# Frequency-domain filter and GELU layer on one core: second weights issued behind batch 1's input, first part of the filters' return at slot 10, last stage of batch 1 two slots later in shorter steps

## The chip, the core and the metric

The kernel runs on one core of a Trainium2 chip. The core has five engines that run side by side and meet only through semaphores: TensorE (PE, matrix products; PEld is its weight load), VectorE (DVE), ScalarE (ACT), GpSimd (POOL) and SyncE (SP). SP and POOL also issue transfers between the device memory and the on-chip memory; 16 DMA engines carry them out. The metric is the device time of one execution in microseconds (us), the median of several runs. Less is better.

## The reference, cut to what matters

Each of 8 batches of 3008 x 256 values goes through a filter in the frequency domain along the sequence; the result goes through two dense layers with an exact GELU between them.

```python
def _attn_ref(x, filt_r, filt_i):          # x: 8 x 3008 x 256
    X = np.fft.rfft(x, axis=1)
    F = (filt_r + 1j * filt_i)[None, :, :]
    return np.fft.irfft(X * F, n=x.shape[1], axis=1)

def _moe_ref(x, w_in, w_out):              # x: 24064 x 256, w_in: 256 x 2048, w_out: 2048 x 256
    h = x @ w_in
    g = 0.5 * h * (1.0 + erf(h * np.float32(1.0 / np.sqrt(2.0))))
    return g @ w_out
```

## The kernel before, in words

The sequence of 3008 is split as 47 x 64, so that the transform becomes four small stages of matrix products, s1 to s4, with a product by the filter F after s2. Between s1 and s2, and between s3 and s4, the data change their layout by a trip through device memory. For batches 1 to 7 the functions are:

- `load_x(b)` (L86): the batch's input, eight transfers issued by POOL, into a single buffer `x_sb`.
- `s1(b, c)`, c = 0 to 3 (L387): reads a quarter of the input. Each quarter reads two of the eight transfers. Results are copied to `a_sb` by DVE and ACT and written to a scratch tensor R by four transfers of SP (L396).
- `r1(b, c)` (L402): reads R back, one transfer of SP a quarter, into `b_sb`. Every r1 needs all sixteen writes of s1.
- `s2(b, p)`, p = 0 to 11 (L410, L413): two products of a pair of frequencies (k = 2p and 2p + 1), then DVE multiplies by F for these k.
- `s3(b, u)` and `s3_out` (L427, L439): three groups of four pairs; the results go to a second scratch tensor by SP.
- `r2(b, c)` (L446): two transfers of SP a quarter, back into `d_sb`.
- `s4(b, grp, half)` (L455, L299): sixteen units; unit u reads quarter u // 4. The results are the batch's sequence, in a ring that the dense layers read.

Batch 0 goes through its own variants (c1 to c4), ahead of everything else.

The dense layers run over 47 tiles of 512 rows. Time is cut into slots, sixteen a tile. In slot s, tile t = s // 16 does one sixteenth of the first product, `mm1` (L569), followed by GELU on ACT (L572), and the tile before does one sixteenth of the second product, `mm2` (L596) or, for most tiles, `mm2_seven` (L657). The latter computes the product with seven quarter products in place of eight; it needs sums of quarters of g (DVE: L627, L633, L640), sums of quarters of w_out (`weight_sums`, POOL, L613), and combines the results on DVE (L670 to L680). `put(slot, f, ...)` writes down by hand that f is issued at the head of a slot; every engine carries out its instructions in the order of issue. The mixing stages of batch b are spread over slots in this way, so that they run beside the dense layers of the batch before. For batch 1 the line

```python
s1, n1, r1, s2, n2, group, r2, s4, n4 = 0, 4, 15, 25, 2.5, 12, 62, 68, 0.72
```

gives: s1 at slots 0, 4, 8 and 12; the first three r1 at 15, the fourth at 33; s2 of pair p at `25 + 12 * (p // 4) + int(2.5 * (p % 4))`, so pairs 0 to 3 at 25 to 32 and pair 4 at 37; the first three r2 at 62; s4 of unit u at `68 + int(0.72 * u)`, that is 68 to 78; the fourth r2 three slots after the first s4. Tile 5 reads batch 1's first rows from slot 80.

Filters: `load_filters` (L95, POOL) loads F as batch 0 needs it, on 64 partitions. `dup_filters` (L113) copies pairs of k to the other 64 partitions. `save_filters` (L99, SP) writes F to the scratch tensor Fd, and `load_filters_again(k0, k)` (L107, SP) brings it back for k0 to k0 + k - 1 in the order of partitions that batches 1 to 7 need: eight transfers of 16 partitions each. The first return is for k 0 to 7 (128 KB a transfer), the second, put at slot 16, for k 8 to 23 (256 KB a transfer).

POOL's order ahead of the slots is: tables, input of batch 0, filters, w_in (L129), copies of F for k 4 to 11, w_out in two halves (`load_w_out`, L133), copies for k 12 to 23, small tables, input of batch 1. Behind that come, at slots 0 to 15, `table_2_parities`, `table_u_pick`, `table_4_rows`, `weights_4`, `weight_sums` and `table_4_all` (L371, L373), and at slot 25 the input of batch 2, not gated.

SP's order is: save of F, first return, sixteen writes of s1, three r1, second return, two stores of the first output tile (L604), the fourth r1, then s3's writes and stores by turns.

The product of batch 0 by F (L499) reads the copies that POOL makes; the product of batch 1 by F (L413) reads the returns. w_out is first read by POOL in `weight_sums` and by PE at slot 16.

Of the kernel before, what the change touches and what calls it, by code (L numbers as in the profile page):

```python
# [693 lines left out]
def kernel(  # L694
# [9 lines left out]
    m = _Mix(ctx, tc, x, filt_r, filt_i, moe_w_in, moe_w_out, out)  # L704
    nc, B, S = tc.nc, m.B, m.S
# [36 lines left out]
    m.load_w_in()  # L742

    nc.gpsimd.memset(m.vt[:, :, 96, :], 0.0)
    m.dup_filters(nc.gpsimd, 4, 8)
    m.load_w_out(0)
    m.load_w_out(8)
    m.dup_filters(nc.gpsimd, 12, 12)
    m.save_filters()


# [52 lines left out]
    m.table_u_rows(g)  # L804
    m.table_1_tiles(g)
    m.load_x(1)
    m.load_filters_again(0, 8)

    warm = g.tile([128, 1], FP32, name="warm")
    nc.scalar.activation(out=warm, in_=m.p, func=AF.Gelu)  # L810
# [11 lines left out]
    def put(slot, f, *a):  # L822
        at.setdefault(slot, []).append((f, a))

    def first(b):
        return (b * S // TCH) * 16

    for b in range(1, B):
        hi = first(b)
        if b == 1:  # L830
            s1, n1, r1, s2, n2, group, r2, s4, n4 = 0, 4, 15, 25, 2.5, 12, 62, 68, 0.72
        else:
            s1, n1, r1, s2, n2, group, r2, s4, n4 = hi - 94, 3.7, hi - 80, hi - 71, 3.4, 14, hi - 25, hi - 17, 1
        unit = lambda p: s2 + group * (p // 4) + int(n2 * (p % 4))
        for u in range(16):
            put(s4 + int(u * n4), m.s4, b, u // 2, u % 2)
        for c in range(4):
            put(s1 + int(c * n1), m.s1, b, c)
            put(r1 if c < 3 else unit(3) + 1, m.r1, b, c)
            put(r2 if c < 3 else s4 + int(4 * n4) + 1, m.r2, b, c)  # L840
        for p in range(12):
            put(unit(p), m.s2, b, p)
            if p % 4 == 3:
                put(unit(p) + 3, m.s3, b, p // 4)
                put(unit(p) + 4, m.s3_out, b, p // 4, 1)
        if b + 1 < B:
            for i in range(8):
                put(unit(i + 2) if b > 1 else 25, m.load_next, b, i + 2, i // 2, i % 2)
# [2 lines left out]
    put(1, m.table_u_pick, g)  # L851
    put(1, m.table_4_rows, g)
    put(1, m.weights_4, g)
    put(16, m.load_filters_again, 8, 16)
    put(4, m.weight_sums)
    put(12, m.table_4_factors, g)
# [48 lines left out]
```

## Time and profile before

| What | Value |
|---|---|
| median of 9 runs | 763.97 us (761.71 to 768.27) |
| profiled execution | 763.81 us, of which span 762.0 us |
| granted TensorE clock, mean | 0.996 |
| busy, share of span: PE / DVE / ACT / POOL | 97% / 76% / 72% / 15% |
| DMA issues F<-Fd: first return / second return | 8 x 128 KB, median 10.2 us to landing / 8 x 256 KB, 13.1 us |
| DMA issue w_out_sb | 2 x 512 KB, median 16.6 us to landing |
| DMA issue Fd<-F | 1 x 1536 KB, 11.3 us to landing |

The span runs from the first to the last instruction in one profiled execution. Busy time is that of the engine; waits and the issue of transfers are not in it. A tag such as `[4.51 <-DMA x_sb<-in_x_dram]` behind a row says how long the engine stood idle before it and what ended that.

### The profile page before, as it was taken

To read this page: it belongs to the slowest core of one execution; us is meant where nothing else is said; L and a number is where in the kernel's file an instruction comes from. 1 tells how busy PE (TensorE), PEld (TensorE's weight loads), DVE (VectorE), ACT (ScalarE), POOL (GpSimd) and SP (SyncE) were. 2 spreads that over 40 slices of the span, in tenths; PEclk is the share of its full clock that TensorE was granted. 3 is DMA by queue.
4 is the path that set the end of the run, shared out by engine and by line. 5 is a ranking of instruction groups with operands and counts; after the bars stand their busy time and mean duration, and the time that the engine had idled before them with its cause. 6 is when DMAs were issued, how large, how long until landed. Compare 5 with 4: busy or idle time off the path is not lost.

```text
span 762.0 us, 20182 instructions
## 1 busy us (share of the span) xinstructions
PE 739.8 (97%) x8388; PEld 518.5 (68%) x8388; DVE 581.8 (76%) x1043; ACT 547.5 (72%) x967; POOL 111.6 (15%) x207
## 2 busy tenths in 40 slices
PE   7969889999999999999999999999999999999998
PEld 4726556666777667676677666766767766777776
DVE  7834887799777986889778897779977799666562
ACT  7867567767787677867778666776678767777773
POOL 7779600012000210002000120001200000000000
PEclk9989999999999999999999999999999999999999
DMA  9998944555624655347535475264562523501011
GB/s 143 223 183 171 195 115 118 161 115 102 166 71 133 147 117 118 92 129 165 119 80 142 134 137 121 79 172 108 108 158 65 148 78 89 134 29 57 29 56 56
DMA packets 91500, 90.70 MB, mean 119 GB/s; under 512 B 7633, under 2 KB 78417, under 8 KB 91089
## 3 DMA queue, kind: packets, MB, share of 16 engines
q1 hardware_dynamic: 83024, 73.43, 36.2%
q0 software_dynamic: 8384, 16.00, 14.3%
q8 instruction: 65, 1.06, 0.6%
q14 instruction: 27, 0.21, 0.1%
HBM read 57.15 MB, written 48.23 MB: 138 GB/s over the span
## 4 chain that ended last, share of the span: by engine, by line
PE 81%; DMA 7%; DVE 6%; POOL 2%; issue 1%; ACT 1%; SPq 0%; DVEq 0%; POOLq 0%; ACTq 0%
PE ps_h L569 37%; PE ps_o L657 33%; DMA x_sb<-in_x_dram 3%; PE ps_s L455 3%; PE ps_s L427 2%; DVE p L413 2%; PE ps_s L387 2%; DVE s_sb L627 2%; PE ps_s L410 2%; DMA d_sb<-R 1%; DMA R<-v_sb 1%; PE ps_o L596 1%; POOL F L113 1%; DMA b_sb<-R 1%; ACT g_sb L572 1%
## 5 line engine op out<-in xcount | busy, mean ns | idle before, releaser
L572 ACT ACTIVATE g_sb<-ps_h 128x512 f16<-128x512 f32 x752 | 448.1, 598 | 187.0 <-PE ps_h L569 184.4
L569 PE MATMUL ps_h<-y_sb,w_in_sb 128*128 128x512 bf16 (+3 forms) x1600 | 447.3, 367 | 1.1 <-ACT g_sb L572 0.6
L657 PEld LDWEIGHTS <-g_sb 128*128 128x128 f16 x2880 | 190.2, 98 | 80.8 <-issue 15.2
L657 PEld LDWEIGHTS <-s_sb 128*128 128x128 f16 x2160 | 147.4, 98 | 51.5 <-issue 3.3
L569 PEld LDWEIGHTS <-w_in_sb 128*128 128x128 bf16 x1600 | 125.0, 98 | 9.7 <-issue 4.4
L657 PE MATMUL ps_o<-w_sums,g_sb 128*128 128x128 f16 x1440 | 125.0, 219 | 1.7 <-DVE g_sb L633 1.5
L657 PE MATMUL ps_o<-w_sums,s_sb 128*128 128x128 f16 x1440 | 124.5, 219 | 0.0
L627 DVE TENSOR_TENSOR s_sb<-g_sb 128x1024 f16<-128x1024 f16 x180 | 120.8, 694 | 0.0
L657 PE MATMUL ps_o<-w_out_sb,g_sb 128*128 128x128 f16 x1440 | 118.4, 219 | 0.4
L413 DVE TENSOR_TENSOR p<-ps_s,F 128x1024 bf16<-128x1024 f32 x84 | 102.6, 1221 | 18.5 <-PE ps_s L410 15.4
L118 POOL COPY gate<-p 1x1 bf16<-1x1 bf16 x40 | 19.4, 484 | 418.6 <-DVE p L413 418.6
L633 DVE TENSOR_TENSOR g_sb<-s_sb,g_sb 128x1024 f16<-128x1024 f16 x90 | 63.1, 701 | 1.1
L657 PE MATMUL ps_o<-w_out_sb,s_sb 128*128 128x128 f16 x720 | 62.2, 219 | 0.0
L640 DVE TENSOR_TENSOR s_sb<-g_sb 128x1024 f16<-128x1024 f16 x90 | 61.4, 682 | 0.0
L297 DVE CAST a_sb<-ps_s 128x512 bf16<-128x512 f32 x56 | 36.1, 686 | 24.7 <-PE ps_s L387 22.9
L299 DVE TENSOR_SCALAR y_sb<-ps_s 128x376 bf16<-128x376 f32 x56 | 30.6, 546 | 31.8 <-PE ps_s L455 31.7
L455 PEld LDWEIGHTS <-d_sb 96*128 96x128 bf16 x448 | 31.3, 98 | 29.0 <-issue 4.4
L675 DVE TENSOR_TENSOR t_sb<-t_sb,ps_o 128x256 f32<-128x256 f32 x45 | 18.7, 417 | 37.9 <-PE ps_o L657 37.8
L672 DVE TENSOR_TENSOR ost<-t_sb,ps_o 128x256 f32<-128x256 f32 x45 | 18.8, 419 | 31.2 <-PE ps_o L657 31.2
L455 PE MATMUL ps_s<-T4a,d_sb 96*128 96x94 bf16 x448 | 37.2, 206 | 3.0 <-DMA d_sb<-R 3.0
L680 DVE TENSOR_TENSOR ost<-t_sb,ps_o 128x256 f32<-128x256 f32 x90 | 33.6, 415 | 6.8 <-PE ps_o L657 6.8
L295 ACT ACTIVATE a_sb<-ps_s 128x512 bf16<-128x512 f32 x56 | 30.6, 608 | 6.3 <-PE ps_s L387 6.3
(149 smaller groups left out, 524.5 us busy)
## 6 DMA issues: line engine op xcount, KB each, us to landing
out_dram<-ost SPq DMA_DIRECT2D x93, 256.0 KB, 2.6
x_sb<-in_x_dram POOLq DMA_DIRECT2D x64, 188.0 KB, 3.9
R<-a_sb SPq DMA_DIRECT2D x112, 96.0 KB, 2.2
b_sb<-R SPq DMA_DIRECT2D x28, 384.0 KB, 4.4
R<-v_sb SPq DMA_DIRECT2D x84, 128.0 KB, 2.5
d_sb<-R SPq DMA_DIRECT2D x56, 192.0 KB, 4.0
F<-Fd SPq DMA_DIRECT2D x8, 256.0 KB, 13.1
Fd<-F SPq DMA_DIRECT2D x1, 1536.0 KB, 11.3
```

The lines of the kernel that those rows point to most:

```text
L295: self.nc.scalar.activation(out=out, in_=in_, func=AF.Copy, scale=1.0 if scale is None else scale)
L297: self.nc.vector.tensor_copy(out=out, in_=in_)
L299: self.nc.vector.tensor_scalar(out=out, in0=in_, scalar1=scale, scalar2=None, op0=ALU.mult)
L413: nc.vector.tensor_tensor(out=w, in0=ps.unsqueeze(1).to_broadcast([128, 2, 512]), in1=self.F[:, :, 2 * p:2 * p + 2, :].rearrange("p t a b ...
L455: nc.tensor.matmul(ps[:, 94 * i:94 * i + 94], lhsT=d[:, (grp % 2) * 4 + i, 128 * half:128 * half + 128], rhs=self.T4a[:, 4 * grp + i], sta ...
L569: nc.tensor.matmul(ps[:, o:o + n], lhsT=self.w_in_sb[:, dc, jc * 128:jc * 128 + 128], rhs=self.ring[:, dc, off:off + n], start=(dc == 0), ...
L572: nc.scalar.activation(out=self.st["g", t][:, jc, :], in_=ps, func=AF.Gelu)
L627: self.nc.vector.tensor_tensor(out=self.st["s", t][:, i:i + 2], in0=a, in1=b, op=ALU.subtract)
L633: self.nc.vector.tensor_tensor(out=a21[:, k], in0=self.st["s", t][:, k, 0], in1=a22[:, k], op=ALU.add)
L640: self.nc.vector.tensor_tensor(out=self.st["s4", t][:, k], in0=a12[:, k], in1=s2[:, k], op=ALU.subtract)
L657: nc.tensor.matmul(ps[:, (m + 1) % 2, sub, :], lhsT=a[:, i, 128 * sub:128 * sub + 128], rhs=b[:, i], start=i == 0, stop=i == 7)
L680: v(out=c(h, 1 - h), in0=tt, in1=p, op=ALU.add)
```

## The change

Three edits. The two halves of w_out are no longer issued between the copies of F but behind the input of batch 1, and the copies become one run of ten. The first return leaves its place behind the input of batch 1 and is put at slot 10; on SP it then stands behind the third group of s1's writes and ahead of the fourth. For batch 1, s4 starts at slot 70 with steps of 0.62, in place of 68 and 0.72: its units go to slots 70 to 79, its fourth r2 to slot 73.

```diff
     nc.gpsimd.memset(m.vt[:, :, 96, :], 0.0)
-    m.dup_filters(nc.gpsimd, 4, 8)
-    m.load_w_out(0)
-    m.load_w_out(8)
-    m.dup_filters(nc.gpsimd, 12, 12)
+    m.dup_filters(nc.gpsimd, 4, 20)
     m.save_filters()
...
     m.load_x(1)
-    m.load_filters_again(0, 8)
+    m.load_w_out(0)
+    m.load_w_out(8)
...
         if b == 1:
-            s1, n1, r1, s2, n2, group, r2, s4, n4 = 0, 4, 15, 25, 2.5, 12, 62, 68, 0.72
+            s1, n1, r1, s2, n2, group, r2, s4, n4 = 0, 4, 15, 25, 2.5, 12, 62, 70, 0.62
...
     put(1, m.weights_4, g)
+    put(10, m.load_filters_again, 0, 8)
     put(16, m.load_filters_again, 8, 16)
```

## The prediction, made before the changed kernel ran

> **What bounds the kernel now.** I read the busy slices of the page first: TensorE (PE) is busy 97% of the 762.0 us span, and the slices below 9 lie in the first sixth. The table by stage then shows which stretches lose time.
>
> ```profile
> core 0: us, PE busy (x) PEld busy (x) DVE busy (x) ACT busy (x) POOL busy (x), PEclk, DMA share, GB/s
> 40.00:50.00 10.00, 4.80 (x20) 1.48 (x24) 1.40 (x3) 2.95 (x6) 7.08 (x22) 0.66 1.12 205
> 110.00:120.00 10.00, 7.80 (x101) 5.77 (x99) 5.38 (x11) 6.01 (x12) 0.00 (x0) 1.00 0.89 208
> ```
>
> Two holes: 5.2 us at 40 to 50, where the granted clock also falls to 0.66 while the DMA engines are full, and 2.2 us at 110 to 120. The PE timeline names what ended each.
>
> ```profile
> 38.24 1.45 PE L546 MATMUL ps_c<-T4c,d_sb 96*128 96x94 bf16 x24
> 44.20 0.60 PE L387 MATMUL ps_s<-x_sb,T1s 47*64 47x512 bf16 x1 [4.51 <-DMA x_sb<-in_x_dram]
> 45.80 1.07 PE L387 MATMUL ps_s<-x_sb,T1s 47*64 47x512 bf16 x7 [0.99 <-DMA x_sb<-in_x_dram]
> ...
> 114.89 0.51 PE L455 MATMUL ps_s<-T4a,d_sb 96*128 96x94 bf16 x8 [2.19 <-DMA d_sb<-R]
> ```
>
> Batch 0's mixing is done at 39.69, and the first matmul of s1 (slot 0) waits 4.51 + 0.99 = 5.50 us for batch 1's input. Slot 68's s4 then waits until its rows are read back. The POOL timeline shows why the input is late.
>
> ```profile
> 22.08 1.79 POOL L133 DMA_DIRECT2D w_out_sb<-in_moe_w_out_dram  x2
> 23.86 5.94 POOL L113 COPY F<-F 64x1024 bf16<-64x1024 bf16 x6
> ...
> 30.86 3.05 POOL L86 DMA_DIRECT2D x_sb<-in_x_dram  x6
> 36.63 0.51 POOL L86 DMA_DIRECT2D x_sb<-in_x_dram  x1 [2.72 <-DMA w_out_sb<-in_moe_w_out_dram]
> 42.27 0.51 POOL L86 DMA_DIRECT2D x_sb<-in_x_dram  x1 [5.14 <-DMA w_out_sb<-in_moe_w_out_dram]
> ```
>
> The input stands behind w_out, which lands 19.0 us after its second issue, at 42.0, and shares the engines with the filters' first return. The last two lines also show that a POOL transfer waits for the landing of the eighth before it. Last, SyncE's queue (SP) and VectorE (DVE):
>
> ```profile
> 34.18 3.66 SPq L107 DMA_DIRECT2D F<-Fd  x8
> 47.78 11.64 SPq L396 DMA_DIRECT2D R<-a_sb  x16
> 61.21 1.30 SPq L402 DMA_DIRECT2D b_sb<-R  x3
> 62.55 6.91 SPq L107 DMA_DIRECT2D F<-Fd  x8
> ```
>
> ```profile
> 24.95 1.23 DVE L499 TENSOR_TENSOR p<-ps_c,F 128x1024 bf16<-128x1024 f32 x1 [0.99 <-POOL F L113]
> ...
> 84.20 1.23 DVE L413 TENSOR_TENSOR p<-ps_s,F 128x1024 bf16<-128x1024 f32 x1 [2.20 <-DMA b_sb<-R]
> 85.34 0.68 DVE L640 TENSOR_TENSOR s_sb<-g_sb 128x1024 f16<-128x1024 f16 x1
> 85.94 0.41 DVE L672 TENSOR_TENSOR ost<-t_sb,ps_o 128x256 f32<-128x256 f32 x1
> 86.39 0.42 DVE L673 TENSOR_TENSOR t_sb<-t_sb,ps_o 128x256 f32<-128x256 f32 x1
> ```
>
> This is the row that decides. The product of pair 4 (slot 37) is the first to read k 8 to 23 of F, so it needs all eight transfers of the second return. The last of these is issued at 69.15 and lands 14.7 us later, at 83.82; DVE starts at 84.20 (the view names b_sb, the next on that semaphore; no data of it is used here). PE resumes slot 43 at 86.96, when L673 frees a bank. Its wait there is only 0.20 us: PE and the filters arrive together. Whatever PE gains earlier it can spend only if the second return lands earlier too. That return starts when SP is through R<-a and b_sb<-R, in order.
>
> **The change, part by part.**
>
> *w_out leaves its place between the copies (L113).* 1.79 us of issue go from POOL. The fifth copy needs the last filter load, issued at 15.41 and landed 7.17 us later (22.58), so it ends near 23.8 instead of 24.92, and DVE, free at 23.96, keeps 0.9 of its 0.99 us wait. Batch 0 ends at 38.8.
>
> *The input comes first.* Eight issues start near 29.9. At 84 us the same eight landed 4.1 to 8.0 us after issue, so the first pair lands near 34.5 and the last near 42; the save of F (landed 34.10) may add some, and 38.8 has 4 us of room. The 5.50 us wait goes. With it goes the cold clock: eight matmuls of L569 took 3.15 us from 46.80, against 1.47 for six a little later. ScalarE, which paces slots 0 to 15, stood idle 0.34 + 0.20 + 0.23 us for it: 0.8. Slots 0 to 12 come 0.9 + 5.5 + 0.8 = 7.2 us earlier.
>
> *w_out behind it.* Its issues wait for the landings of the first two input loads (near 35); behind them in POOL's order stand T2p, the pick tables, weights_4, weight_sums, table_4_all and the input of batch 2. Its 1 MB follows the input: at the 176 GB/s that the DMA view shows for 33 to 38 us, 6 us, landed near 48. First use: slot 16, 59.2 - 7.2 = 52.0. That cover is 4 us; if w_out were later, PE would lose the excess. weight_sums (10 us) then ends near 58 and table_4_all (24 us) near 82, due only above 110: free. The input of batch 2 then starts at 82 instead of 83.99 and meets the end of the second return: 0.2 us, at most 1.
>
> *First return at slot 10.* Eight issues at 0.43 us move from a gap of SP's queue to between the third and fourth group of R<-a. Behind them wait the last four R<-a (each also for the landing of a return, by the eighth-before rule), b_sb<-R, the second return, two stores and b_sb's fourth part. The third group's issue ends at 57.4 - 7.2 = 50.2, so the first return moves data from about 51.7 for a time T. The fourth group's data are ready by 50.3, but its rows go behind: from its last issue (58.98) to b_sb's (61.21) the trace has 2.2 us, I take 2.1. b_sb<-R then starts at 51.7 + T + 2.1 = 53.8 + T, against 61.21, and the second return's end moves by as much.
>
> T is not in the trace undisturbed. Upper bound: before, beside the input, first and last landed at 41.4 and 50.7, eight in 9.3 x 8/7 = 10.6 us. Lower: 1.05 MB at the fastest stretch below, 331 GB/s, 3.2 us, but the last issue (53.8) plus the shortest landing (2.2) makes it 4.3. The nearest row is the second return, same form, twice the size:
>
> ```profile
> 62.50:65.00 2.50, 2.50 (x19) 1.69 (x18) 0.00 (x0) 1.69 (x4) 2.34 (x4) 1.00 0.90 331
> ...
> 71.00:74.00 3.00, 3.00 (x25) 2.12 (x23) 3.00 (x4) 1.87 (x4) 2.92 (x3) 1.00 0.99 134
> 74.00:77.00 3.00, 3.00 (x40) 1.91 (x42) 3.00 (x4) 2.10 (x4) 2.84 (x4) 1.00 1.01 137
> ```
>
> Alone on full engines it runs at 134 to 137 GB/s: 1.05/0.137 = 7.6 us, which I take. So b_sb<-R starts at 61.4, 0.2 later than before, and the 7.2 us are spent: PE would wait at slot 25 (ready 59.8, data 61.4 + 3.1 = 64.5; a lower clock after it, as at 40 to 50, would be hidden by the next wait) and again at slot 43.
>
> [...]
>
> *s4 from slot 70.* Slots before it take 0.82 us (L569 at 111.27 and 112.10). Slot 68 is reached at 112.53 and waits to 114.89; slot 70 is reached 1.64 us later with useful work done, so 1.64 of 2.36 us are saved. No DMA moves but the fourth d_sb pair (slot 73 for 71), due at slot 77. At 1.6 units a slot PE does 0.82 + 1.6 x 0.17 = 1.1 us, ACT 0.60 + 0.8 x 0.48 = 1.0: PE still paces. The last unit moves to slot 79, one before the ring is read: 1.4 us of PE work against 1.1 us of ScalarE: 0, at worst 0.4.
>
> **Sum.** Against the 762.0 us span: 0.2 (gate) + 0.2 (batch 2's input) - 1.64 = -1.25. In general T - 8.85. The profiled run took 763.81 (1.8 us around the span), the median is 763.97, so 762.7.
>
> **Rivals.**
> *The return is cheap.* If its packets spread like b_sb's, T = 4.3 and the sum is -4.5: 759.4. For it: the engines are half free around slot 10 (45% in the DMA view for 54 to 57 us). Against: 134 GB/s at share 0.99 with nothing beside it.
> *The return blocks SP (slower).* If it runs at its own old pace or worse, T is from 10.6 to 15.1 (16.6 us from first issue to last landing before, less 1.5), 12.8 in the middle: +4.0, 768.0. It decides as soon as T passes 8.85, that is, when b_sb<-R starts after 62.6. For it: w_out may still be landing, and the fourth group waits on the return twice. Against: the input that it shared with is then gone.
> *The input is still late.* If the save of F holds it to 45.8, nothing moves forward: b_sb<-R starts at 57.4 + 1.5 + 7.6 + 2.1 = 68.6, 7.4 late, less 1.4: 770. Against: between 31 and 33 us the DMA view shows slices at 0.1 to 0.7 busy, room for it.
>
> **Numbers.** About 0.3%, 2.3 us, is what a measurement can tell from no change: 761.7 to 766.3. My case 0.52 (its own range 761.0 to 764.5 for T of 6 to 9.4), cheap return 0.26, blocked SP 0.18, late input 0.04. Faster is the cheap return and a quarter of my case, 0.39; slower is most of the last two, 0.18; the same 0.43. The range 758.6 to 767.2 reaches to the cheap return and most of the way to the blocked queue.
>
> **What would show it.** No DMA wait before L387 near 39; the fifth copy ends by 24; first return 50 to 60; b_sb<-R issued at 61 to 62; a PE wait of some 4 us at slot 25, new; DVE's fifth product near 84 as before; a wait under 1 us before the first s4. If b_sb<-R is issued before 59, or the fifth product starts before 82, T was too large; if that product no longer waits for F at all, the argument itself is wrong and the gain is up to 9 us.

## The result, and the profile after

| What | Before | After |
|---|---|---|
| median | 765.44 us (53 runs, 760.39 to 769.13) | 761.22 us (16 runs, 757.41 to 764.35) |
| ratio, 95% interval | 1 | 0.9944 [0.9929, 0.9960] |
| profiled execution / its span | 763.81 / 762.0 us | 760.71 / 758.9 us |

Before is here the kernel before as it was run beside the changed one. A ratio and its interval are taken over all runs of the two kernels, so a ratio can differ by up to 0.1% from that of the two medians; what is said below to be gained in us is the ratio's. The change took 4.3 us (3.1 to 5.4) off. The same kernel run again in a later group gave 0.9963 [0.9946, 0.9980], 2.8 us. Both ratios pass the 0.3% that can be told from no change, though not by much, and the second interval reaches down to 0.2%. The forecast of 762.7 us, 1.25 us less than before, named the right mechanism and was some 1.5 to 3 us too high; the outcome that it gave the best chance, no change that can be told (0.43, against 0.39 for faster), did not come.

The table by stage first (us from the start, then the busy time of each engine, the granted clock, the busy share of the DMA engines and what they moved):

```profile
core 0: us, PE busy (x) PEld busy (x) DVE busy (x) ACT busy (x) POOL busy (x), PEclk, DMA share, GB/s
40.00:50.00 10.00, 7.58 (x49) 2.67 (x49) 3.87 (x6) 9.21 (x21) 6.01 (x20) 0.95 1.13 206
50.00:60.00 10.00, 10.00 (x61) 6.02 (x59) 0.69 (x1) 6.97 (x13) 9.84 (x16) 0.88 0.93 148
60.00:70.00 10.00, 7.17 (x42) 4.57 (x41) 4.27 (x5) 3.46 (x7) 9.45 (x12) 0.83 0.98 206
110.00:120.00 10.00, 8.93 (x121) 6.80 (x120) 5.04 (x11) 6.87 (x13) 0.00 (x0) 1.00 0.92 210
```

The hole at 40 to 50 has shrunk: PE is busy 7.58 us there, 4.80 before, at a clock of 0.95 in place of 0.66. A new one stands at 60 to 70, with 7.17 us of PE. The hole at 110 to 120 has lost 1.1 us. The DMA engines have a busy share of 0.93 or more from 40 to 70. In the kernel before they had room in two of these three stretches (0.62 and 0.86):

```profile
50.00:60.00 10.00, 8.54 (x58) 3.44 (x55) 3.87 (x6) 9.93 (x24) 10.00 (x18) 1.00 0.62 149
60.00:70.00 10.00, 10.00 (x71) 6.85 (x70) 2.55 (x3) 6.81 (x12) 9.45 (x13) 1.00 0.86 193
```

PE's timeline after the change names the waits:

```profile
36.41 1.45 PE L546 MATMUL ps_c<-T4c,d_sb 96*128 96x94 bf16 x24
37.79 0.63 PE L387 MATMUL ps_s<-x_sb,T1s 47*64 47x512 bf16 x8
...
48.58 0.22 PE L351 MATMUL ps_t<-eye,T1g 47*96 47x47 bf16 x2 [1.64 <-ACT a_sb L295]
...
63.10 0.61 PE L410 MATMUL ps_s<-b_sb,T2p 128*128 128x256 bf16 x2 [2.83 <-DMA b_sb<-R]
...
85.16 0.38 PE L657 MATMUL ps_o<-w_sums,g_sb 128*128 128x128 f16 x4 [1.77 <-DVE t_sb L673]
...
113.61 0.51 PE L455 MATMUL ps_s<-T4a,d_sb 96*128 96x94 bf16 x8 [1.07 <-DMA d_sb<-R]
```

s1 (L387) follows batch 0 with no wait for the input: 5.50 us of waiting are gone. Then come waits that were shorter or not there: 2.83 us for batch 1's rows at slot 25 (none before) and 1.77 us at slot 43 for a bank that DVE frees (0.20 before), beside 1.64 us at slot 12 (0.81 before; the reason for that one is below). The wait ahead of the first s4 went from 2.19 to 1.07 us. SP's queue and DVE's timeline show what the first two of these waits wait for:

```profile
39.56 9.48 SPq L396 DMA_DIRECT2D R<-a_sb  x12
49.15 3.68 SPq L107 DMA_DIRECT2D F<-Fd  x8
52.92 2.75 SPq L396 DMA_DIRECT2D R<-a_sb  x4
59.78 1.30 SPq L402 DMA_DIRECT2D b_sb<-R  x3
61.17 5.23 SPq L107 DMA_DIRECT2D F<-Fd  x8
```

```profile
17.48 11.40 DVE L499 TENSOR_TENSOR p<-ps_c,F 128x1024 bf16<-128x1024 f32 x10
47.95 1.29 DVE L297 CAST a_sb<-ps_s 128x512 bf16<-128x512 f32 x2 [2.83 <-DMA R<-a_sb]
...
63.75 1.22 DVE L413 TENSOR_TENSOR p<-ps_s,F 128x1024 bf16<-128x1024 f32 x1 [4.05 <-DMA b_sb<-R]
...
82.41 1.23 DVE L413 TENSOR_TENSOR p<-ps_s,F 128x1024 bf16<-128x1024 f32 x1 [3.78 <-PE ps_s L410]
```

Three quarters of the rows' writes are issued by 49.0 and have landed by 50.9. The fourth is issued from 52.92 on, behind the first return, whose eight transfers land some 0.95 us apart, the last at 59.02; only then is b_sb read, at 59.78, against 61.21 before. The second return follows and lands its last part at 82.03, and the fifth product starts at 82.41, against 84.20. (The view names PE at that row; PE's product, at 76.74, had long been done, and the landing 0.4 us earlier is the one that fits.) So of the time won in front, little is left by then:

| us from the start | Before | After | Earlier by |
|---|---|---|---|
| mm1 of slot 12 | 57.30 | 48.83 | 8.5 |
| b_sb<-R issued | 61.21 | 59.78 | 1.4 |
| last landing of the second return | 83.82 | 82.03 | 1.8 |
| fifth product of DVE (pair 4) | 84.20 | 82.41 | 1.8 |
| mm1 of slot 43 | 87.18 | 85.38 | 1.8 |
| mm1 of slot 80 | 127.99 | 125.06 | 2.9 |
| end of the span | 762.05 | 758.89 | 3.2 |

The differences from b_sb<-R to slot 43 are hardly larger than those between two executions of one kernel. In the profile of s4_only, a run told below whose kernel is that of before up to slot 67, b_sb<-R is issued at 59.83 and the fifth product comes as early as in the change (that execution took 760.26 us, 3.8 less than the median of its kernel):

```profile
82.47 1.22 DVE L413 TENSOR_TENSOR p<-ps_s,F 128x1024 bf16<-128x1024 f32 x1 [1.99 <-PE ps_h L569]
```

In a second profile of the change it comes at 83.88. So what is won in front is not shown to be worth anything at slot 43.

### The profile page after: what moved, and what is told of

Its sections match the earlier page's. It is cut to its first block, busy times and chain, and to the rows that moved or that the text cites. A ratio compares the mean times of both kernels' runs of the same rounds, so it can differ in the third digit from the quotient of the medians.

```text
span 758.9 us, 20181 instructions
## 1 busy us (share of the span) xinstructions
PE 740.6 (98%) x8388; PEld 519.0 (68%) x8388; DVE 580.6 (77%) x1043; ACT 547.5 (72%) x967; POOL 111.7 (15%) x207
## 4 chain that ended last, share of the span: by engine, by line
PE 82%; DMA 7%; DVE 6%; ACT 2%; issue 1%; SPq 1%; POOL 0%; DVEq 0%; ACTq 0%; POOLq 0%
PE ps_h L569 37%; PE ps_o L657 33%; PE ps_s L455 3%; PE ps_s L427 2%; DVE p L413 2%; PE ps_s L410 2%; PE ps_s L387 2%; DMA R<-a_sb 2%; DVE s_sb L627 2%; DMA F<-Fd 1%; DMA b_sb<-R 1%; PE ps_o L596 1%; DMA d_sb<-R 1%; DMA R<-v_sb 1%; ACT y_sb L295 1%
## 5 line engine op out<-in xcount | busy, mean ns | idle before, releaser
L410 PE MATMUL ps_s<-b_sb,T2p 128*128 128x256 bf16 x168 | 32.3, 274 | 2.9 <-DMA b_sb<-R 2.8
```

The lines of the kernel that those rows point to most:

```text
L410: nc.tensor.matmul(ps[:, 256 * i:256 * i + 256], lhsT=self.T2p[:, k].rearrange("p a b c d -> p (a b c d)"), rhs=self.st[b, "b", k // 6][:, ...
```

## The experiments

Three groups were run, each beside the kernel before on its own chip (medians 764.59, 764.04 and 764.18 us). Ratios are to those. The theory: the filters' return costs its full 7.6 us in front of b_sb<-R, and takes back what the input gave. The rivals: the return is cheap or at the wrong place, or the gain comes from s4 alone.

**Each part by itself.** First, s4's slots alone.

```diff
-            s1, n1, r1, s2, n2, group, r2, s4, n4 = 0, 4, 15, 25, 2.5, 12, 62, 68, 0.72
+            s1, n1, r1, s2, n2, group, r2, s4, n4 = 0, 4, 15, 25, 2.5, 12, 62, 70, 0.62
```

> The kernel before with the third edit alone (s4 of batch 1 at slots 70 to 79). Gate theory (the second return's last landing holds everything up to slot 43, the s4 wait is a separate hole): 1.1 to 1.6 us faster than before, the first s4 starts near 114.9 as before, its wait falls from 2.2 to under 1 us, nothing else moves. Rival (the rows are read back when PE asks for them, so the wait moves along): 0.

764.05 us, 0.9993 [0.9974, 1.0012]: 0.5 us less, with 1.5 either way. In its profile the first s4 waits 1.02 us in place of 2.19. This run does not tell whether the change is more than this edit: by its interval the edit can be worth up to 2.0 us, by the second measurement of the change the whole is worth 1.5 to 4.1. Next, on the kernel before, the return at slot 10 alone:

```diff
     m.load_x(1)
-    m.load_filters_again(0, 8)
...
+    put(10, m.load_filters_again, 0, 8)
```

> The kernel before with the second edit alone (first return at slot 10, w_out left in its place, s4 at 68). Gate theory: the input lands some 4 us earlier because the return no longer shares the engines with it, but SP now carries 7.6 us of return between the third and fourth group of rows; b_sb<-R starts at 64 to 66 instead of 61.2 and the kernel is 2 to 4 us slower than before. Front theory (the gain is the input wait removed, the returns are hidden): 3 to 5 us faster than before.

765.19 us, 1.0018 [0.9999, 1.0037], 1.4 us more, which its interval just fails to tell from none. With the return no longer beside the input, s1 waits 4.2 us less for it (1.32 in place of 5.50), yet b_sb<-R went out at 63.37, 2.2 later than before. Without w_out's move the step brings nothing and, if anything, costs more than it brings, by rather less than expected.

**The change without the s4 edit,** beside the change itself once more.

```diff
-            s1, n1, r1, s2, n2, group, r2, s4, n4 = 0, 4, 15, 25, 2.5, 12, 62, 70, 0.62
+            s1, n1, r1, s2, n2, group, r2, s4, n4 = 0, 4, 15, 25, 2.5, 12, 62, 68, 0.72
```

> The changed kernel with s4 of batch 1 back at slots 68 to 78. If the third edit carries its 1.4 to 1.9 us (from DVE's fifth product to the end of the span: 676.5 with it, 677.9 without): 1.4 to 1.9 us slower than the changed kernel of the same group, first s4 after a wait of 2 us or more. If the third edit is worth what its run alone showed between the runs (0.5 us): the same as the changed kernel.

> The changed kernel once more, as the yardstick of this group: 3 to 5 us faster than before, DVE's fifth product near 82.5, second return's last landing near 82.

The change 761.89 us, 0.9963 [0.9946, 0.9980]; without the s4 edit 763.97 us, 0.9995 [0.9978, 1.0013]. So w_out and the return together are worth nothing that shows (from 1.7 us less to 1.0 more), and the 2.1 us between the two medians are the s4 edit's in this place. PE's timeline of the one without it has the old wait again, 2.12 us:

```profile
113.76 0.51 PE L455 MATMUL ps_s<-T4a,d_sb 96*128 96x94 bf16 x8 [2.12 <-DMA d_sb<-R]
```

The edit gave 0.5 us alone and 2.1 in the whole, against 1.64 forecast; the two intervals overlap, and these runs don't part them. The profiles are steadier behind the front: from DVE's fifth product to the end of the span the kernel before takes 677.85 us, the change 676.48 and 676.21 in its two profiles and s4 alone 675.98, so 1.4 to 1.9 less. (The kernel of the row above takes 679.17; the mean granted clock of that execution was 0.993, against 0.995 to 0.996 in the other four.)

**No first return at all.** It moves 1 MB less and leaves out part of the computation, as its expectation says.

```diff
-    put(10, m.load_filters_again, 0, 8)
```

> The changed kernel without the first return (the first 8 values of k keep batch 0's arrangement for batches 1 to 7, so pairs 0 to 3 of these batches use the wrong filter rows; 1 MB of transfers is left out). Gate theory: T = 0; b_sb<-R starts near 52, the second return's last landing near 74, 8 us earlier; PE no longer waits at slot 25; what DVE and PE need by themselves then bounds, and the kernel is 5 to 8 us faster than the changed kernel (9 to 12 faster than before). Front theory: the return is hidden, within 1 us of the changed kernel.

755.08 us, 0.9884 [0.9860, 0.9907]: 8.9 us under before, and 6.1 to 6.8 under the change (761.22, 761.89). DVE's timeline:

```profile
60.29 1.23 DVE L413 TENSOR_TENSOR p<-ps_s,F 128x1024 bf16<-128x1024 f32 x1 [0.83 <-PE ps_s L410]
...
77.92 1.22 DVE L413 TENSOR_TENSOR p<-ps_s,F 128x1024 bf16<-128x1024 f32 x1 [3.21 <-DMA R<-v_sb]
```

The product at 60.29 waits only 0.83 us, for PE, and the fifth comes at 77.92, 4.5 us before the change's; b_sb<-R is issued at 54.37, 5.4 before it. This is the return's price, and the input's gain is seen once it is gone. The fifth product still waits 3.21 us: the second return is late by itself. Its last landing, at 77.55, is the one that fits that row, though the view names another; 74 was expected for it, and 52 for b_sb<-R.

**Another place for the return.** Ahead of slot 0, behind w_out, where it was before relative to s1; then at slot 13, behind all of s1's writes:

```diff
     m.load_w_out(8)
+    m.load_filters_again(0, 8)
...
-    put(10, m.load_filters_again, 0, 8)
```

> The changed kernel with the first return put back ahead of slot 0, behind w_out in the order of issue (on SP it is then the first behind the save of F). Gate theory: the first return shares the engines with the input at 32 to 42 us, both are slower than alone but faster than one after the other (before, the return ran at some 100 GB/s beside the input, 75% of its pace alone); the input's first pair lands by 39 at the latest; SP's queue is free for the rows, b_sb<-R starts at 53 to 56, the second return's last landing is at 75 to 78 and the kernel is 3 to 6 us faster than the changed kernel, 7 to 10 us faster than before, less what w_out, which lands at 52 or later, costs at slot 16 (0 to 3 us). Front theory (the return has to be away from the input for the gain): the input is late again and the time goes back towards the kernel before, 0 to 2 us faster than before.

```diff
-    put(10, m.load_filters_again, 0, 8)
+    put(13, m.load_filters_again, 0, 8)
```

> The changed kernel with the first return at slot 13, behind the fourth group of rows in SP's order and ahead of b_sb<-R. Gate theory, refined by the traces (the rows that stand behind the return wait for its landing, and b_sb<-R is issued only then, so the engines have nothing for SP from the return's last landing to the first data of b_sb): here b_sb<-R is issued at 54 to 57 and its data follow the return's at once, landing at 60 to 61.5 in place of 63; the second return ends near 80 in place of 82 to 83.5, and the kernel is 2 to 3 us faster than the changed kernel (5 to 7 faster than before). Rival (what counts is the sum of bytes ahead, in whatever order): the same as the changed kernel.

In both the theory's gain over the change (3 to 6 us and 2 to 3) failed to come: 761.55 us, 0.9967 [0.9949, 0.9984], and 761.67 us, 0.9970 [0.9955, 0.9985], the same as the change. For slot 13 that is what the rival said: the sum of the bytes ahead counts, in whatever order. SP's queue of the early one, and PE's timeline of it:

```profile
33.00 4.11 SPq L107 DMA_DIRECT2D F<-Fd  x8
41.04 15.41 SPq L396 DMA_DIRECT2D R<-a_sb  x16
59.57 1.29 SPq L402 DMA_DIRECT2D b_sb<-R  x3
```

```profile
53.07 0.28 PE L351 MATMUL ps_t<-eye,T1g 47*96 47x47 bf16 x2 [4.36 <-ACT a_sb L295]
```

The return is out of b_sb's way, but now it moves beside the input and w_out, w_out lands at 57.69 in place of 47.65, and s1's sixteen writes, which move beside w_out, take 15.41 us to issue. ACT and DVE can't reuse a_sb until those land, and PE waits 4.36 us. b_sb<-R goes out at 59.57, as in the change at 59.78. With slot 13 the queue and PE look like this:

```profile
51.64 3.66 SPq L107 DMA_DIRECT2D F<-Fd  x8
55.40 2.07 SPq L402 DMA_DIRECT2D b_sb<-R  x3
58.05 7.88 SPq L107 DMA_DIRECT2D F<-Fd  x8
```

```profile
62.52 0.39 PE L410 MATMUL ps_s<-b_sb,T2p 128*128 128x256 bf16 x2 [3.44 <-DMA b_sb<-R]
```

b_sb<-R is issued 4.4 us earlier, but lands at 62.48, since the return's data are still moving; the second return ends at 82.16 (82.03 in the change). In each order the same bytes pass through engines whose busy share is 0.92 or more in every ten us from 40 to 70, and the second return ends at 82.0 to 83.0 (83.5 in the second profile of the change). That pointed away from the place and to the rate.

**A faster return.** The 131 GB/s of the return are far from the 206 GB/s of the stages about it. What sets the pace could be its 16 partitions, or its rows (every second one of Fd). F is saved in the order in which it is wanted (four transfers in place of one), and each return becomes four transfers of 32 partitions:

```diff
-        self.nc.sync.dma_start(out=self.Fd, in_=self.F[0:64])
+        for par in range(2):
+            for q in range(2):
+                o, i = 32 * par + 16 * q, 32 * q + (par ^ q)
+                self.nc.sync.dma_start(out=self.Fd[o:o + 16], in_=self.F[i:32 * q + 32:2])
...
-                for q in range(2):
-                    o = 64 * par + 32 * r + 16 * q
-                    self.nc.sync.dma_start(out=self.F[o:o + 16, :, k0:k0 + k, :],
-                                           in_=self.Fd[32 * q + (par ^ q):32 * q + 32:2, :, k0:k0 + k, :])
+                o = 64 * par + 32 * r
+                self.nc.sync.dma_start(out=self.F[o:o + 32, :, k0:k0 + k, :],
+                                       in_=self.Fd[32 * par:32 * par + 32, :, k0:k0 + k, :])
```

> The changed kernel with F saved in the order in which it is wanted (four transfers of 16 partitions) and returned in four transfers of 32 partitions in place of eight of 16; bytes and places in SP's order are the same. Gate theory: the returns are held by how few partitions they write (134 GB/s at full share of the engines); the first return takes 4 to 5 us in place of 7.6, the second 8 to 10 in place of 15.2, its last landing falls to 72 to 75; DVE's fifth product no longer waits for F, and 4 to 6 us go off the changed kernel (8 to 10 us faster than before), as without the first return. Rival (the pace is that of the device memory or of the engines, whatever the partitions): landings as in the changed kernel, no change beside it.

753.11 us, 0.9861 [0.9833, 0.9888]: 10.6 us under before, faster than both kernels, and at least as fast as the one with no first return (0.9884). Its tables by stage, where the second return is what moves, then the change's for its second return:

```profile
66.00:70.00 4.00, 4.00 (x40) 2.77 (x38) 4.00 (x5) 2.57 (x5) 3.77 (x5) 1.00 1.03 219
```

```profile
72.00:76.00 4.00, 4.00 (x49) 2.26 (x47) 3.96 (x6) 2.50 (x5) 3.84 (x4) 1.00 1.03 131
```

219 GB/s against 131 in the last two columns, at the same share of 1.03: here a full DMA share does not tell at what pace the engines move. In these two stretches of 4 us the engines took up 107 packets of 8 KB against 64. The last landing of the second return is at 72.70, 9.3 us earlier, and DVE's fifth product (the same line of code, 415 here) has no wait left:

```profile
73.78 1.27 DVE L299 CAST v_sb<-ps_s 128x512 bf16<-128x512 f32 x2
74.97 1.21 DVE L415 TENSOR_TENSOR p<-ps_s,F 128x1024 bf16<-128x1024 f32 x1
```

DVE's timeline shows no wait from 63.09 to this row, where the change's has one of 3.78 us: DVE's own work bounds here now, not the filters.

**Which half of that edit does it.** The sorted save, but again eight transfers of 16 partitions, now of adjoining rows:

```diff
-                o = 64 * par + 32 * r
-                self.nc.sync.dma_start(out=self.F[o:o + 32, :, k0:k0 + k, :],
-                                       in_=self.Fd[32 * par:32 * par + 32, :, k0:k0 + k, :])
+                for q in range(2):
+                    o, i = 64 * par + 32 * r + 16 * q, 32 * par + 16 * q
+                    self.nc.sync.dma_start(out=self.F[o:o + 16, :, k0:k0 + k, :],
+                                           in_=self.Fd[i:i + 16, :, k0:k0 + k, :])
```

> Saved in the wanted order as in the runs with 32 partitions, but returned in eight transfers of 16 partitions again, first return at slot 10. If the partitions set the pace: 134 GB/s again, a landing of the second return every 1.9 to 2.0 us, its last near 82 to 84, and the time of the changed kernel (2 to 4 us faster than before). If the order in the device memory (rows read in sequence) or the save made the gain: landings as with 32 partitions, 10 us faster than before.

761.93 us, 0.9973 [0.9957, 0.9988]: all of the gain is gone. The second return lands one transfer every 2.06 us and ends at 83.58, and the table by stage has 127 GB/s:

```profile
70.00:74.00 4.00, 4.00 (x37) 2.82 (x35) 4.00 (x5) 2.46 (x5) 3.76 (x5) 1.00 1.02 127
```

So neither the save nor the order of the rows counts. Nor is it that four transfers, each twice as large, take the place of eight: at the same 256 KB a transfer, those of 16 partitions land 2.0 us apart (second return of the change), those of 32 partitions 1.16 us apart (first return of the wide kernel, landings from 52.88 to 56.37). What counts is the 32 partitions of a transfer.

**The wide return with other orders.** On the kernel before, with none of the three edits; and on the change with the return early, or at slot 13 (diffs as above).

> The kernel before with save and returns of 32 partitions, none of the three edits. Gate theory: the second return ends at 73 to 76 in place of 83.8, DVE's fifth product starts without a wait for F, but the input's wait of 5.5 us at 39 to 46 stays (somewhat shorter, 3 to 5 us, as the first return leaves the engines sooner) and so does that of s4: 2 to 5 us faster than before, 5 to 8 us slower than the changed kernel with the same returns. So the input's wait is worth its full size only where the returns no longer hold. Rival (the input's wait was all that counted): as before.

> The kernel with the first return ahead of slot 0, with saves and returns as in the run beside it (four saves in the wanted order, returns of 32 partitions). Gate theory: the first return costs the input less time, w_out still lands late (55 or so) and holds the first rows' writes; within 2 us of the run beside it, and 4 to 6 us faster than the changed kernel. Rival: as the early return with 16 partitions, 2 to 3 us faster than before.

> The same place with the returns of 32 partitions. There DVE's fifth product no longer waits for F, and only the wait of 1.6 us at slot 25 is left to win: 0.5 to 2 us faster than with slot 10 (752 or less in the median where slot 10 gave 753.1).

On the kernel before: 761.90 us, 0.9965 [0.9944, 0.9986], 2.7 us. Early: 755.70 us, 0.9882 [0.9857, 0.9908], 1.6 us behind slot 10 by the ratios, within the 2 that were expected. Slot 13: 753.82 us, 0.9853 [0.9831, 0.9875], the same as slot 10, where 0.5 to 2 us less were expected. PE's timeline of the first shows why the wide return alone brings little:

```profile
40.91 0.37 PE L389 MATMUL ps_s<-x_sb,T1s 47*64 47x512 bf16 x1 [0.49 <-DMA x_sb<-in_x_dram]
42.35 1.06 PE L389 MATMUL ps_s<-x_sb,T1s 47*64 47x512 bf16 x7 [1.07 <-DMA x_sb<-in_x_dram]
```

The late input still holds s1 back there, though by less (42.35 in place of 45.80). The three edits, worth 2.8 to 4.3 us with the narrow return, are worth 7.9 us with the wide one (0.9861 against 0.9965, from two groups). Between the two profiles it is 5.7 us: slot 12 comes 4.4 us earlier, DVE's fifth product 2.5, and 3.2 come behind that, s4's edit among them. So more than half of what the step in front wins is kept once no return takes it back.

## Why the prediction was right, and where its sizes were off

- *w_out between the copies; the input first.* As forecast. The ten products of batch 0 run without a wait (row at 17.48), s1 starts at 37.79, and slots 0 to 12 come 8.5 us earlier, 7.2 forecast. Of the 1.3 between, 0.7 are there from the outset, before any edit acts: the first product of batch 0's c2 stands at 15.81 in this profile and at 16.55 in that of before.
- *w_out behind the input.* Landed at 47.65, near 48 as forecast. Not foreseen: it moves beside the first writes of s1. Their first group, issued at 39.56, landed 6.0 us later (4.0 before); that is behind the 2.83 us of DVE and the 1.64 us of PE above. What it cost the end no run separates: the first return stands behind these writes in SP's queue.
- *First return, T = 7.6.* Right: the eight land 6.64 us from first to last, so 7.6 for eight, at 138 GB/s, 137 taken. The new wait at slot 25 is 2.83 us for 4 forecast, DVE's fifth product 82.41 for 84.
- *The tail behind it, 2.1: the term that failed.* The four writes of the fourth group landed 0.18 us apart, and b_sb<-R went out 0.76 us after the return's last landing (59.02 to 59.78), 0.99 in the second profile of the same kernel, and 0.71 to 0.91 in the profiles of three more kernels with the return at slot 10. The 2.1 came from a stretch in which the writes were issued as they became ready; here they had been waiting. That is 1.1 to 1.3 us, of the order of the 1.5 to 3 us by which the runs beat the forecast of 1.25. That the time falls by as much is not shown: without s4's edit the other two left 0.4 us, 1.3 either way.
- *s4.* Slot 43 to slot 80 takes 1.1 us less in the profile, the fifth product to the end 1.4 to 1.9, 1.64 forecast, 0.5 to 2.1 in the runs: right in size, though the runs alone leave it wide. The wait left is 1.07, "under 1 us" forecast.
- *Batch 2's input.* Begins at 80.62 (83.99 before), for 82 forecast; nothing more of it was measured.
- *By the profile:* the forecast had slot 43 later by 0.4 and it came 1.8 earlier (2.2: 1.3 the tail, 0.3 a return that, by its landings, began to move at 51.4 and not 51.7, 0.4 a second return that took 22.25 us from b_sb's issue to its end and not 22.61, 0.2 batch 2's input, which was not felt), s4 gave 0.5 less, and 0.2 more came after slot 80: -1.25 - 2.2 + 0.5 - 0.2 = -3.15, the span's -3.2. In the second profile b_sb<-R is at 61.33 and the fifth product at 83.88, within 0.2 us of the forecast, and the span (760.1) 1.9 less; and in the profile of s4_only, whose front is that of before, the fifth product is at 82.47. The 1.8 us at slot 43 thus lie within what one execution differs from another by, and this sum tells of one pair of profiles only.
- *Rivals.* The cheap return is out (T = 7.6). The blocked queue is out: b_sb<-R was issued before 62.6, though the return's move alone on the kernel before, where the input gave less, put it at 63.37 (its time, 1.4 us more, is just within the noise). The input was not late.

One reading went beyond the forecast: the 134 to 137 GB/s had been taken as what full engines give. They were the pace of a 16-partition transfer, and the largest gain lay there.

## What to carry to other kernels

When a load is moved forward, add up what the queue behind it must still move before the next common wait: here the return, the rows and the second return passed one after the other, and 8.5 us won at slot 12 were at most 1.8 at slot 43; with the return elsewhere the second one ended within 1 us of the same time. When several orders of the same transfers end at one time, change the rate, not the order: compare the GB/s of the stretch with that of its neighbours at the same busy share, and look at how many partitions each transfer touches (here 131 GB/s with 16, 219 with 32). And two steps can be worth more together than the sum of what each is worth alone: 2.7 us for the wide return alone, 2.8 to 4.3 for the three edits, 10.6 for both.

## What the runs showed of the chip

- A return of 16 partitions a transfer ran at 127 to 138 GB/s in the three kernels shown (before, after, the sorted save), one of 32 partitions at 219, both at a busy share of the DMA engines of 0.99 to 1.03.
- Writes of one queue stood behind the packets of another. Between 39.6 and 43.0 us of the change the engines moved 1214 packets, nearly all of them 512 B of w_out on POOL's queue and none of SP's; the first write of s1, issued by SP at 39.56, landed 6.0 us after issue, 4.0 in the kernel before beside the end of the input, and about 2 there for the second group. With w_out and the return both in flight SP needed 15.41 us to issue sixteen, 11.64 before. Whether w_out's small packets or its bytes do this, no run separates.
- The granted clock of PE fell to one half for 3.4 us twice, behind the 1.64 us at slot 12 and around the end of the 2.83 us at slot 25:

```profile
49.00:52.50 3.50, 3.50 (x11) 1.44 (x10) 0.24 (x1) 2.72 (x9) 3.50 (x7) 0.51 0.94 180
52.50:62.70 10.20, 7.77 (x54) 4.99 (x51) 0.69 (x1) 5.81 (x10) 9.89 (x14) 1.00 0.84 153
62.70:66.10 3.40, 3.00 (x13) 1.83 (x14) 1.22 (x1) 0.60 (x1) 3.24 (x5) 0.50 1.18 303
```

- In the 3.4 us ahead of the first of these two stretches (45.6 to 49.0) PE was busy for 1.57 us, ahead of the second (59.3 to 62.7) for 0.97 us. In the profile of before the clock stood at 0.50 once, from 42.53 to 49.36 us, and PE had been busy for 0.51 us of the 3.4 ahead of that (39.1 to 42.5). What makes the clock fall no run separates.
- The clock goes with the spread of the runs. Of the 29 runs of the kernel before in the last group, twelve had a mean granted clock of 0.993 and a median of 764.52 us, thirteen 0.996 and 763.03. The wide return on the change ran at 0.998 to 1.000, so a part of its 10.6 us may go with the clock; how much no run separates.
